# An FFT filter with a bilinear layer behind it on one core: the projection one step later, casts of g behind later products, transform loads three deep

## The chip, the core and the metric

One core of a Trainium2 chip runs the whole program. The metric is the time of one execution in device microseconds (us). The kernel before takes 2731.31 us, the median of three runs (2729.96 to 2734.04).

Engines are named as in the profile: PE is TensorE's matmul, PEld its weight load, DVE is VectorE, ACT is ScalarE, POOL is GpSimd, SP is SyncE, which issues most of the DMAs. Each engine works through its own list of instructions in order, and semaphores tie the lists together.

## What is computed

```python
def _attn_ref(x, filt_r, filt_i):          # x: (8, 3072, 256)
    X = np.fft.rfft(x, axis=1)
    F = (filt_r + 1j * filt_i)[None, :, :]
    Y = X * F
    return np.fft.irfft(Y, n=x.shape[1], axis=1).astype(np.float32)

def _moe_ref(x, w_a, w_b, w_out):          # x: (8 * 3072, 256), w_a, w_b: (256, 1536)
    a = x @ w_a
    b = x @ w_b
    return (a * b @ w_out).astype(np.float32)
```

A long convolution along the sequence (a real FFT, a product with a filter, the inverse FFT), then two first layers, multiplied with each other, and a projection back to 256 columns.

## The kernel before

**Numbers in two parts.** Operands of matmuls are of type fp32r, whose mantissa is cut. To keep precision an operand is held as a high part, cast by ACT, and a low part, the rest that POOL (in places DVE) subtracts. One product is then three matmuls: high with high, high with low, low with high. In the code the parts end in `h` and `l` (`gh`, `gl`, `xh`, `xl`).

**The transforms.** 3072 is 128 x 24. Per batch the forward transform has 12 pieces `s1` (a DFT over 128 rows, from tiles `xt` and a table `st`), whose results go out to DRAM (`store_z`), and 16 pieces `s2` (a DFT over 24, from tiles `zt` read back), each with the filter on DVE: four instructions that make `y`, `v` and `y+v`. The inverse has 16 pieces `is1` (from the halves `yh`, `yl` that `split_y` makes) and per chunk two pieces `is2`, whose results are cast into `ah`, `al`, the operand of the first layers.

**The steps.** The loop runs over 8 batches, 6 chunks `c` of 512 rows, and 6 pairs `p` of column blocks of 128: 288 steps. A step is numbered by its slot, 12c + 2p, from 0 to 70 within a batch. In it, seven products of Strassen's scheme (`product`, numbers 1, 2, 5, 6, 7, 3, 4 in this order, six matmuls of 256 columns each) build both first layers in three PSUM banks x, y, z. ACT copies and DVE additions gather them in `c0` (for block f0) and `c1` (for block f1). `parts` multiplies both layers to `g` on DVE; `split` casts it to `gh` (ACT) and subtracts to `gl` (POOL); `project` multiplies the halves with `w_out` into the banks `po0`, `po1`, 12 matmuls for each of f0 and f1. So a step holds 66 matmuls of 256 columns. `store` copies the two `po` banks to `ot` (two DVE copies) when a chunk's last projection is done.

**The order.** It is written out by hand in the step's code below; nothing reorders it. In the middle of a step, between products 6 and 7, stands the projection of the step before's f0, in front of product 4 that of its f1. `plan` and `early` are tables from slots to pieces of the transforms for the next batch: the even slot's `plan` runs after product 3, the odd slot's in the middle of the next step (`after`), and `early` (the casts `split_x`, `split_y`) also in the middle. In batches 1 to 6, `s1` pieces lie in slots 3 to 25, `s2` in 30 to 60, `is1` in 33 to 63; batch 7 has no transforms to prepare but `is2`. In batch 0 the `s1` pieces come twice as densely (slots 14 to 25), behind a start-up that converts the weights (`more_weights`).

**Buffers that matter.** `c0` and `c1` exist once; ACT's copy of product 5 into `c1[:, 1]` (L727) must therefore wait until DVE's `parts` of the step before's f1 (L567) has read `c1`. Bank x alternates between two, y and z exist once. ACT's copy of product 1 (L720) has to be done before product 6 may write into the same bank, that of product 6 (L729) before product 7. `xt`, `st` and `zt` have two buffers each.

Of the kernel before, what the change touches and what calls it, by code (L numbers as in the profile page):

```python
# [22 lines left out]
NP = NF // 2  # L23
# [174 lines left out]
def fft_filter_bilinear_kernel(ctx: ExitStack, tc, x, filt, fny, wa, wb, wo, s1c, gc, fc, fl, ic, sc, s1f, ff, fi, out):  # L198
# [141 lines left out]
    def load_x(b, i):  # L340
        n0, n1 = PAIRS[i]
        xt = later[0].tile([128, 2, D], F32, name="xt", tag="xt", bufs=2)
        nc.sync.dma_start(out=xt, in_=x[b].rearrange("(p n) d -> p n d", n=N2)[:, n0:n1 + 1:n1 - n0])
        held["x", b, i] = xt

    def load_s(b, i):
        st = later[0].tile([128, 2, 2, 128], F32R, name="st", tag="st", bufs=2)
        nc.sync.dma_start(out=f32(st), in_=s1d[i])
        held["s", b, i] = st
# [9 lines left out]
    def s1(b, i):  # L359
        (xh, xl), st = held.pop(("xs", b, i)), held.pop(("s", b, i))  # L360
        ps = ps_f.tile([128, 2, D], F32, name="ps", tag="ff")
        for n in range(2):
            for q, (w, m) in enumerate(((0, xh), (0, xl), (1, xh))):
                nc.tensor.matmul(ps[:, n], st[:, n, w], m[:, n], start=q == 0, stop=q == 2)  # L364
        zh = later[0].tile([128, 2, D], F32R, name="zh", tag="zh")
        zl = later[0].tile([128, 2, D], F32R, name="zl", tag="zl")
        nc.scalar.copy(out=zh, in_=ps)
        nc.vector.tensor_tensor(out=zl, in0=ps, in1=f32(zh), op=ALU.subtract)
        held["zs", b, i] = zh, zl
# [15 lines left out]
    def load_z(b, i):  # L385
        zt = later[0].tile([128, 2, 2, D], F32R, name="zt", tag="zt")
        for h, r in ((0, 128), (1, 96)):
            zv = zd[b][h].rearrange("(j q) n d -> j (q n) d", q=4)[2 * i:2 * i + 2]
            nc.sync.dma_start(out=f32(zt[0:r, h]), in_=zv.rearrange("j p d -> p j d"))
        held["z", b, i] = zt  # L390
# [12 lines left out]
    def s2(b, i):  # L403
        zt, fr, fm = held.pop(("z", b, i)), filts[2 * (i % 2)], filts[2 * (i % 2) + 1]
        ps = ps_f.tile([128, 2, D], F32, name="ps", tag="ff")
        turn(i, fct, flt, zt[:, 0], zt[0:96, 1], ps)
        y = later[0].tile([128, 2, D], F32, name="y", tag="y")
        v = later[0].tile([128, 2, D], F32, name="v", tag="v", bufs=1)
        nc.vector.scalar_tensor_tensor(out=y, in0=ps, scalar=sct[:, 0:1], in1=fr, op0=ALU.mult, op1=ALU.mult)  # L409
# [10 lines left out]
    def split_y(b, i):  # L420
        y = held["y", b, i]
        yh = later[0].tile([128, 2, D], F32R, name="yh", tag="yh", bufs=1)
        yl = later[0].tile([128, 2, D], F32R, name="yl", tag="yl", bufs=1)
        nc.scalar.copy(out=yh, in_=y)
        nc.gpsimd.tensor_tensor(out=yl, in0=y, in1=f32(yh), op=ALU.subtract)
        held["y", b, i] = yh, yl

    def is1(b, i):
        ps = ps_f.tile([128, 2, D], F32, name="ps", tag="ff")
        turn(i, ict, ict, *held.pop(("y", b, i)), ps[0:96])  # L430
        t = later[0].tile([96, 2, D], F32, name="t", tag="t", bufs=1)
# [132 lines left out]
    def parts(r, g, tag):  # L564

        gt = moe[0].tile([128, 2, 256], F32, name="g", tag="g" + tag)
        nc.vector.tensor_tensor(out=gt, in0=g[:, :, 0], in1=g[:, :, 1], op=ALU.mult)  # L567
        gh = moe[0].tile([128, 2, 256], F32R, name="gh", tag="gh" + tag)
        gl = moe[0].tile([128, 2, 256], F32R, name="gl", tag="gl" + tag)
        r[tag] = gh, gl, gt  # L570

    def split(r, tag):
        gh, gl, gt = r[tag]
        nc.scalar.copy(out=gh, in_=gt)  # L574
# [24 lines left out]
    with tc.manual_schedule():  # L599
# [56 lines left out]

        last, after = None, []
        for b in range(B):
# [15 lines left out]
            if b + 1 < B:  # L674
                at(o, start_batch, b + 1)
                for i in range(2):
                    at(o, load_x, b + 1, i)
                for i in range(2):
                    at(o, load_s, b + 1, i)
                for i in range(NI):  # L680
# [4 lines left out]
                    at(t + 3 if b == 0 else t + 4, store_z, b + 1, i)  # L685
                    if i + 2 < NI:
                        at(t + 2 if b == 0 else t + 3, load_s, b + 1, i + 2)
                        at(t + 2, load_x, b + 1, i + 2)
                t = 26 if b == 0 else 28
                for i in range(2):  # L690
                    at(t - 2, load_f, i)
                at(t, load_z, b + 1, 0)
                at(t, load_z, b + 1, 1)
                for i in range(NJ):
                    t = 30 + 2 * i
                    at(t, s2, b + 1, i)
                    if i + 2 < NJ:
                        at(t, load_z, b + 1, i + 2)
                    if i + 2 < NJ:
# [13 lines left out]
            for c in range(NC):  # L713
                for p in range(NP):
                    slot = NF * c + 2 * p
                    r = {"at": (b, c, p)}
                    bx, by, bz = bank("x"), bank("y"), bank("z")
                    c0 = moe[0].tile([128, 2, 2, 256], F32, name="c0", tag="c0")
                    product(b, c, p, 1, bx, True)
                    nc.scalar.copy(out=c0[:, 0], in_=bx)  # L720
                    product(b, c, p, 2, by, True)
                    if last:
                        parts(last, last["c1"], "f1")
                    nc.vector.tensor_tensor(out=c0[:, 0], in0=by, in1=c0[:, 0], op=ALU.add)
                    product(b, c, p, 5, bz, True)
                    c1 = r["c1"] = moe[0].tile([128, 2, 2, 256], F32, name="c1", tag="c1")
                    nc.scalar.copy(out=c1[:, 1], in_=bz)  # L727
                    product(b, c, p, 6, bx)
                    nc.scalar.copy(out=c0[:, 1], in_=bx)  # L729
                    if last:  # L730
                        split(last, "f1")
                    for what, at_slot in after:
                        run(what, at_slot)
                    run(early, slot)
                    if last:
                        project(last, 0)
                    product(b, c, p, 7, bx)
# [3 lines left out]
                    parts(r, c0, "f0")  # L741
                    split(r, "f0")
                    run(plan, slot)
                    if last:
                        project(last, 1)
                        if p == 0:
                            store(*last["at"][:2])
                    product(b, c, p, 4, bx)
                    nc.scalar.copy(out=c1[:, 0], in_=bx)  # L749
                    after = [(plan, slot + 1), (early, slot + 1)]  # L750
                    if p == NP - 1:
                        del held["t", b, c]
                    last = r
        parts(last, last["c1"], "f1")
        split(last, "f1")
        project(last, 0)
        project(last, 1)
        store(*last["at"][:2])

# [33 lines left out]
```

## Time and profile before

| | |
|---|---|
| median of three runs | 2731.31 us |
| the profiled execution itself | 2729.53 us |
| its span in the trace | 2727.7 us |
| PE busy | 2611.6 us, 96% of the span |
| DVE busy | 1779.0 us, 65% |
| ACT busy | 1362.5 us, 50% |
| POOL busy | 1234.9 us, 45% |
| granted TensorE clock, mean | 0.986 |

Matmuls are pipelined: a matmul of 256 columns is listed with 0.28 us, but the next one starts 0.117 us after it. PE's idle time in the trace counts only from the modelled end of the matmul before, so a step's loss is better read from its length than from the idle times.

### The profile page before, as it was taken

The page shows a single profiled execution, that of the slowest core. Times are in us where ns is not written, and L with a number is a line of the kernel's source. Part 1 is how long each engine was busy: PE and PEld are TensorE (multiplying, and loading weights), DVE is VectorE, ACT ScalarE, POOL GpSimd, SP SyncE. Part 2 cuts the span into 40 slices and gives each one's busy share as a digit, 9 for nine tenths or more (in the row PEclk, how much of TensorE's full clock was granted, in tenths as well). Part 3 has the DMA queues.
Part 4 walks back from the last instruction along what each step waited for, and adds up shares of the span by engine and source line. Part 5 has one row for each costly group of instructions (what it writes and reads, how often), then busy time and mean ns, then how long its engine had stood idle before and what let it go on. Part 6 is the DMA issues. An engine that isn't in the chain of part 4 may idle for free.

```text
span 2727.7 us, 53145 instructions
## 1 busy us (share of the span) xinstructions
PE 2611.6 (96%) x20920; PEld 2522.9 (92%) x20920; DVE 1779.0 (65%) x2552; ACT 1362.5 (50%) x2483; POOL 1234.9 (45%) x948
## 2 busy tenths in 40 slices
PE   5688999999999999999999999999999999999999
PEld 2388999999999999999999999999999999999998
DVE  6674676557765577556775567655776557755555
ACT  4454455545545454555455545455454555544443
POOL 4464444444444444444444544454444444533433
PEclk7899999999999999999999999999999999999999
DMA  8435442344414443243432344234441444310100
GB/s 267 141 110 187 150 135 67 111 159 123 131 52 144 138 131 106 82 146 128 141 101 82 132 150 139 75 101 161 129 130 51 143 136 132 112 46 20 40 20 17
DMA packets 206813, 311.27 MB, mean 114 GB/s; under 512 B 20673, under 2 KB 120578, under 8 KB 206482
## 3 DMA queue, kind: packets, MB, share of 16 engines
q1 hardware_dynamic: 149986, 228.16, 26.6%
q10 hardware_dynamic: 56576, 79.71, 8.5%
q8 instruction: 164, 2.69, 0.4%
q14 instruction: 87, 0.71, 0.1%
HBM read 202.93 MB, written 108.45 MB: 114 GB/s over the span
## 4 chain that ended last, share of the span: by engine, by line
PE 80%; DVE 9%; ACT 4%; issue 3%; DMA 2%; ACTq 1%; POOL 1%; SPq 0%; POOLq 0%; DVEq 0%
PE x L556 27%; PE po L587 26%; PE z L556 13%; PE y L556 6%; PE ps L525 3%; DVE g L567 3%; PE ps L364 2%; PE ps L398 2%; PE ps L399 2%; DVE v L411 1%; ACT c L729 1%; DVE c L740 1%; ACT gh L574 1%; DVE c L738 1%; DVE y L409 1%
## 5 line engine op out<-in xcount | busy, mean ns | idle before, releaser
L575 POOL TENSOR_TENSOR gl<-g,gh 128x512 fp32r<-128x512 f32 x576 | 757.3, 1315 | 1296.8 <-ACT gh L574 1247.5
L567 DVE TENSOR_TENSOR g<-c 128x512 f32<-128x512 f32 x576 | 553.5, 961 | 266.9 <-ACT c L749 216.6
L574 ACT CAST gh<-g 128x512 fp32r<-128x512 f32 x576 | 359.9, 625 | 702.2 <-DVE g L567 699.4
L587 PE MATMUL po<-woh,gl 128*128 128x256 f32 x2304 | 650.5, 282 | 14.4 <-POOL gl L575 14.4
L587 PE MATMUL po<-woh,gh 128*128 128x256 f32 x2304 | 658.0, 286 | 0.7 <-ACT gh L574 0.2
L587 PE MATMUL po<-wol,gh 128*128 128x256 f32 x2304 | 645.6, 280 | 0.0
L587 PEld LDWEIGHTS po<-woh,gl 128*128 128x128 f32 x2304 | 434.4, 189 | 20.6 <-POOL gl L575 20.5
L587 PEld LDWEIGHTS po<-woh,gh 128*128 128x128 f32 x2304 | 435.4, 189 | 19.2 <-DVE ot L595 10.1
L587 PEld LDWEIGHTS po<-wol,gh 128*128 128x128 f32 x2304 | 435.4, 189 | 6.6
L738 DVE TENSOR_TENSOR c<-x,c 128x512 f32<-128x512 f32 x288 | 198.3, 689 | 316.0 <-PE x L556 314.0
L556 PE MATMUL x<-ah,wah 128*128 128x256 f32 x1152 | 334.5, 290 | 41.5 <-ACT c L729 21.7
L727 ACT COPY c<-z 128x512 f32<-128x512 f32 x288 | 169.3, 588 | 392.0 <-DVE g L567 265.7
L556 PE MATMUL x<-ah,wbl 128*128 128x256 f32 x1152 | 323.9, 281 | 0.0
L556 PE MATMUL x<-al,wbh 128*128 128x256 f32 x1152 | 323.8, 281 | 0.0
L556 PE MATMUL x<-al,wah 128*128 128x256 f32 x1152 | 323.6, 281 | 0.0
L556 PE MATMUL x<-ah,wbh 128*128 128x256 f32 x1152 | 323.3, 281 | 0.0
L556 PE MATMUL x<-ah,wal 128*128 128x256 f32 x1152 | 322.9, 280 | 0.0
L556 PEld LDWEIGHTS x<-ah,wah 128*128 128x128 f32 x1152 | 218.0, 189 | 56.9 <-ACT c L729 30.9
L556 PEld LDWEIGHTS x<-al,wah 128*128 128x128 f32 x1152 | 218.9, 190 | 0.0
L556 PEld LDWEIGHTS x<-ah,wal 128*128 128x128 f32 x1152 | 218.1, 189 | 0.0
L556 PEld LDWEIGHTS x<-ah,wbl 128*128 128x128 f32 x1152 | 217.7, 189 | 0.0
L556 PEld LDWEIGHTS x<-ah,wbh 128*128 128x128 f32 x1152 | 217.7, 189 | 0.0
(120 smaller groups left out, 5980.4 us busy)
## 6 DMA issues: line engine op xcount, KB each, us to landing
filt<-in_filt SPq DMA_DIRECT2D x336, 128.0 KB, 2.8
z<-zh ACTq DMA_DIRECT2D x112, 256.0 KB, 2.4
zt<-z SPq DMA_DIRECT2D x112, 256.0 KB, 2.9
td<-t ACTq DMA_DIRECT2D x128, 192.0 KB, 2.1
out<-ot SPq DMA_DIRECT2D x48, 512.0 KB, 2.7
tt<-td SPq DMA_DIRECT2D x47, 512.0 KB, 4.1
xt<-in_x SPq DMA_DIRECT2D x84, 256.0 KB, 2.9
st<-s1d SPq DMA_DIRECT2D x84, 256.0 KB, 2.7
```

Of the source, the lines that this page charges most:

```text
L364: nc.tensor.matmul(ps[:, n], st[:, n, w], m[:, n], start=q == 0, stop=q == 2)
L398: nc.tensor.matmul(ps[:, j:2], w[:, 0], hi[:, j:2], start=True, stop=False)
L399: nc.tensor.matmul(ps[:, j:2], wl[:, 0], lo[:, j:2], start=False, stop=True)
L409: nc.vector.scalar_tensor_tensor(out=y, in0=ps, scalar=sct[:, 0:1], in1=fr, op0=ALU.mult, op1=ALU.mult)
L525: nc.tensor.matmul(ps[:, n], tt[:, n, 128 * k:128 * k + 128], gt[:, n], start=True, stop=True)
L556: nc.tensor.matmul(bank[:, k], w[:, m], v[:, n], start=first and k == 0 and q == 0, stop=q == 2, skip_group_check=True)
L567: nc.vector.tensor_tensor(out=gt, in0=g[:, :, 0], in1=g[:, :, 1], op=ALU.mult)
L574: nc.scalar.copy(out=gh, in_=gt)
L575: nc.gpsimd.tensor_tensor(out=gl, in0=gt, in1=f32(gh), op=ALU.subtract)
L587: nc.tensor.matmul(o, g[:, n], w[p][:, f], start=p == 0 and f == 0 and n % 2 == 0 and q == 0, stop=p == NP - 1 and f == 1 and q == 2, skip ...
L727: nc.scalar.copy(out=c1[:, 1], in_=bz)
L738: nc.vector.tensor_tensor(out=c1[:, 1], in0=bx, in1=c1[:, 1], op=ALU.add)
```

## The change

The projection lags further: where step r held the projections of r-1 (f0 in the middle, f1 near the end), it now holds f1 of step r-2 in the middle and f0 of step r-1 near the end. `split` of f0 is moved from the end of its own step to behind product 2 of the next; `split` of f1 is moved behind the middle's transform pieces and behind the projection there. `c1` gets two buffers. `store` moves from the end of a chunk's first step to the middle of its second. The loads `xt`, `st` and the two halves of `zt` (now separate tiles) share a ring of six buffers of 2 KB and are issued three pieces ahead instead of two; `zh`, `y` and `zl`, `v`, `t` share two rings of two (`e1`, `e2`), `yh`, `yl` the buffers of `xh`, `xl`.

```diff
@@ load_x, load_s
-        xt = later[0].tile([128, 2, D], F32, name="xt", tag="xt", bufs=2)
+        xt = later[0].tile([128, 2, D], F32, name="xt", tag="ld", bufs=6)
...
-        st = later[0].tile([128, 2, 2, 128], F32R, name="st", tag="st", bufs=2)
+        st = later[0].tile([128, 2, 2, 128], F32R, name="st", tag="ld", bufs=6)
@@ load_z
-        zt = later[0].tile([128, 2, 2, D], F32R, name="zt", tag="zt")
+        zt = []
         for h, r in ((0, 128), (1, 96)):
+            zt.append(later[0].tile([r, 2, D], F32R, name=f"zt{'hl'[h]}", tag="ld", bufs=6))
             zv = zd[b][h].rearrange("(j q) n d -> j (q n) d", q=4)[2 * i:2 * i + 2]
-            nc.sync.dma_start(out=f32(zt[0:r, h]), in_=zv.rearrange("j p d -> p j d"))
+            nc.sync.dma_start(out=f32(zt[h]), in_=zv.rearrange("j p d -> p j d"))
@@ s2, is1
-        v = later[0].tile([128, 2, D], F32, name="v", tag="v", bufs=1)
+        v = later[0].tile([128, 2, D], F32, name="v", tag="e2")
...
-        t = later[0].tile([96, 2, D], F32, name="t", tag="t", bufs=1)
+        t = later[0].tile([96, 2, D], F32, name="t", tag="e2")
@@ parts, split
+        r[tag] = gt
+
+    def split(r, tag):
+        gt = r[tag]
         gh = moe[0].tile([128, 2, 256], F32R, name="gh", tag="gh" + tag)
         gl = moe[0].tile([128, 2, 256], F32R, name="gl", tag="gl" + tag)
-        r[tag] = gh, gl, gt
-
-    def split(r, tag):
-        gh, gl, gt = r[tag]
+        r[tag] = gh, gl
@@ the plan of the loads
-                    if i + 2 < NI:
-                        at(t + 2 if b == 0 else t + 3, load_s, b + 1, i + 2)
-                        at(t + 2, load_x, b + 1, i + 2)
+                    if i + 3 < NI:
+                        at(t + 2 if b == 0 else t + 3, load_x, b + 1, i + 3)
+                        at(t + 2 if b == 0 else t + 3, load_s, b + 1, i + 3)
...
-                    if i + 2 < NJ:
-                        at(t, load_z, b + 1, i + 2)
+                    if i + 3 < NJ:
+                        at(t, load_z, b + 1, i + 3)
@@ the step
+                    c1 = r["c1"] = moe[0].tile([128, 2, 2, 256], F32, name="c1", tag="c1", bufs=2)
...
                     product(b, c, p, 2, by, True)
-                    if last:
-                        parts(last, last["c1"], "f1")
+                    if prev:
+                        split(prev[-1], "f0")
+                        parts(prev[-1], prev[-1]["c1"], "f1")
...
                     nc.scalar.copy(out=c0[:, 1], in_=bx)
-                    if last:
-                        split(last, "f1")
                     for what, at_slot in after:
                         run(what, at_slot)
                     run(early, slot)
-                    if last:
-                        project(last, 0)
+                    if len(prev) == 2:
+                        one = prev.pop(0)
+                        project(one, 1)
+                        if one["at"][2] == NP - 1:
+                            store(*one["at"][:2])
+                    if prev:
+                        split(prev[-1], "f1")
                     product(b, c, p, 7, bx)
...
                     parts(r, c0, "f0")
-                    split(r, "f0")
                     run(plan, slot)
-                    if last:
-                        project(last, 1)
-                        if p == 0:
-                            store(*last["at"][:2])
+                    if prev:
+                        project(prev[-1], 0)
@@ behind the loop
+        one, r = prev
+        split(r, "f0")
+        parts(r, r["c1"], "f1")
+        split(r, "f1")
+        project(one, 1)
+        project(r, 0)
+        project(r, 1)
+        store(*r["at"][:2])
```

How the rows stand on the engines, at the places that matter. First ACT in the step of slot 48 of batch 3 (c = 4, p = 0), from the copy of product 4 before it to the one at its end; L720/L722, L727/L729, L729/L731 and L749/L751 copy products 1, 5, 6 and 4. Before:

```order
L749 COPY c1_16024<-x_15996 128x512
L720 COPY c0_16128<-x_16125 128x512
L727 COPY c1_16153<-z_16127 128x512
L729 COPY c0_16128<-x_16125 128x512
L574 CAST gh_16144<-g_16142 128x512
L432 COPY t_16167<-ps_16164 96x512
L434 DMA td_13403<-t_16167 96x2x256
L424 CAST yh_16170<-y_16094 128x512
L574 CAST gh_16202<-g_16200 128x512
L749 COPY c1_16153<-x_16125 128x512
```

And after, the same step:

```order
L751 COPY c1_16046<-x_16042 128x512
L722 COPY c0_16175<-x_16172 128x512
L576 CAST gh_16190<-g_16135 128x512
L729 COPY c1_16176<-z_16174 128x512
L731 COPY c0_16175<-x_16172 128x512
L433 COPY t_16214<-ps_16211 96x512
L435 DMA td_13435<-t_16214 96x2x256
L425 CAST yh_16217<-y_16140 128x512
L576 CAST gh_16233<-g_16194 128x512
L751 COPY c1_16176<-x_16172 128x512
```

The cast for f0 went from in front of the last copy of its step to between the copies of products 1 and 5 of the next; the cast for f1 went behind the transform's `t` and `yh`.

POOL around the step of slot 46 (p = 5) and the next, with the two subtractions `al` of the chunk's `is2`. Before:

```order
L575 TENSOR_TENSOR gl_16016<-g_16013,gh_16015 128x512
L545 TENSOR_TENSOR al_15684<-t_15921,ah_15683 128x512 x2
L425 TENSOR_TENSOR yl_16056<-y_15965,yh_16055 128x512
L575 TENSOR_TENSOR gl_16088<-g_16085,gh_16087 128x512
L575 TENSOR_TENSOR gl_16145<-g_16142,gh_16144 128x512
```

After:

```order
L577 TENSOR_TENSOR gl_16061<-g_16005,gh_16060 128x512
L546 TENSOR_TENSOR al_15727<-t_15966,ah_15726 128x512 x2
L426 TENSOR_TENSOR yl_16102<-y_16010,yh_16101 128x512
L577 TENSOR_TENSOR gl_16118<-g_16064,gh_16117 128x512
L577 TENSOR_TENSOR gl_16191<-g_16135,gh_16190 128x512
```

On POOL the kinds stand in the same sequence; the `gl` ahead of `al` is now an f0, the one behind `yl` an f1.

DVE at the start of a chunk's second step (slot 50), where L567/L568 is `parts`, L595/L597 the copies of `store` and L738/L743 the addition of product 7. Before:

```order
L567 TENSOR_TENSOR g_16200<-c0_16128 128x512
L409 SCALAR_TENSOR_TENSOR y_16209<-ps_16206,sct_114,filt2_120 128x512
L411 SCALAR_TENSOR_TENSOR v_16210<-ps_16206,sct_114,filt3_121 64x512 x2
L417 TENSOR_TENSOR y_16209<-y_16209,v_16210 128x512
L595 COPY ot_16233<-po0_15566 128x512
L595 COPY ot_16233<-po1_15567 128x512
L567 TENSOR_TENSOR g_16261<-c1_16153 128x512
L724 TENSOR_TENSOR c0_16247<-y_16245,c0_16247 128x512
L738 TENSOR_TENSOR c1_16272<-x_16244,c1_16272 128x512
```

After:

```order
L568 TENSOR_TENSOR g_16251<-c0_16175 128x512
L410 SCALAR_TENSOR_TENSOR y_16256<-ps_16253,sct_114,filt2_120 128x512
L412 SCALAR_TENSOR_TENSOR v_16257<-ps_16253,sct_114,filt3_121 64x512 x2
L418 TENSOR_TENSOR y_16256<-y_16256,v_16257 128x512
L568 TENSOR_TENSOR g_16310<-c1_16176 128x512
L727 TENSOR_TENSOR c0_16291<-y_16289,c0_16291 128x512
L597 COPY ot_16349<-po0_15656 128x512
L597 COPY ot_16349<-po1_15657 128x512
L743 TENSOR_TENSOR c1_16292<-x_16288,c1_16292 128x512
```

The two copies of `store` went from ahead of `parts` of f1 to behind it and behind the addition of product 2.

## Rows read from the trace of the kernel before

**Rows 1.** Page: PE's busy time, share and count; granted clock in 40 slices.

```profile
PE 2611.6 (96%) x20920; PEld 2522.9 (92%) x20920; DVE 1779.0 (65%) x2552; ACT 1362.5 (50%) x2483; POOL 1234.9 (45%) x948
...
PEclk7899999999999999999999999999999999999999
```

**Rows 2.** Waits of PE over the span: us in total, times, longest.

```profile
PE x L556 <- ACT c L729: 21.7, 44, 1.3
PE po L587 <- POOL gl L575: 14.4, 23, 0.8
PE x L556 <- ACT c L720: 12.9, 15, 2.2
...
PE ps L364 <- POOL xl L356: 4.5, 4, 2.8
```

**Rows 3.** Windows, batch 3: slots 36, 38, 40, 48, 50, 60, 62, 64; then slots 36-46.

```profile
core 0: us, PE busy (x) PEld busy (x) DVE busy (x) ACT busy (x) POOL busy (x), PEclk, DMA share, GB/s
1286.66:1296.54 9.88, 9.27 (x73) 8.66 (x71) 8.10 (x10) 4.41 (x9) 6.60 (x5) 1.00 0.35 105
1296.54:1306.48 9.94, 9.22 (x72) 8.46 (x71) 8.04 (x12) 4.32 (x9) 3.90 (x3) 1.00 0.48 154
1306.48:1315.18 8.70, 8.70 (x73) 8.50 (x71) 6.86 (x10) 4.42 (x9) 3.90 (x3) 1.00 0.69 218
1343.10:1353.38 10.28, 9.28 (x73) 8.68 (x71) 8.50 (x11) 4.44 (x9) 7.00 (x5) 1.00 0.34 101
1353.38:1363.34 9.96, 9.25 (x73) 8.50 (x71) 8.05 (x12) 4.35 (x9) 3.90 (x3) 1.00 0.50 157
1399.95:1410.21 10.26, 9.26 (x72) 8.67 (x71) 8.51 (x11) 4.45 (x9) 6.98 (x5) 1.00 0.07 21
1410.21:1419.89 9.68, 9.00 (x71) 8.15 (x69) 7.79 (x11) 4.19 (x8) 3.88 (x3) 1.00 0.21 74
1419.89:1428.10 8.21, 8.21 (x70) 8.10 (x69) 3.96 (x5) 4.01 (x8) 2.58 (x2) 1.00 0.13 31
...
1286.66:1343.10 56.44, 55.10 (x439) 52.94 (x438) 43.66 (x62) 28.76 (x53) 26.37 (x21) 1.00 0.44 136
```

**Rows 4.** Timeline, batch 3, slots 46 to 48: start, us, instruction, idle before and releaser.

```profile
1336.67 0.59 ACT L727 COPY c<-z 128x512 f32<-128x512 f32 x1 [1.69 <-DVE g L567]
...
1339.12 0.59 ACT L538 CAST ah<-ps 128x512 fp32r<-128x512 f32 x1 [0.38 <-PE po L587]
...
1341.49 3.08 POOL L545 TENSOR_TENSOR al<-t,ah 128x512 fp32r<-128x512 f32 x2 [1.87 <-ACT ah L544]
1344.54 1.29 POOL L425 TENSOR_TENSOR yl<-y,yh 128x512 fp32r<-128x512 f32 x1
1345.79 1.72 POOL L575 TENSOR_TENSOR gl<-g,gh 128x512 fp32r<-128x512 f32 x1
...
1346.30 1.75 DVE L567 TENSOR_TENSOR g<-c 128x512 f32<-128x512 f32 x1
...
1347.56 0.38 PE L587 MATMUL po<-woh,gl 128*128 128x256 f32 x1 [0.74 <-POOL gl L575]
...
1348.14 0.59 ACT L727 COPY c<-z 128x512 f32<-128x512 f32 x1 [3.04 <-DVE g L567]
```

**Rows 5.** Timeline of DVE, batch 3, slot 38: the copies of the store.

```profile
1299.28 1.29 DVE L595 COPY ot<-po 128x512 f32<-128x512 f32 x2
```

**Rows 6.** Windows, batch 2, the steps of slots 16 and 24.

```profile
873.45:881.95 8.50, 8.50 (x75) 8.50 (x74) 4.29 (x6) 4.40 (x9) 3.85 (x3) 1.00 0.60 210
...
909.64:919.41 9.77, 8.77 (x74) 8.56 (x73) 5.28 (x8) 4.74 (x9) 5.65 (x5) 1.00 0.21 82
```

**Rows 7.** Timeline of ACT, batch 2, slots 22 to 24.

```profile
910.43 0.62 ACT L574 CAST gh<-g 128x512 fp32r<-128x512 f32 x1 [2.07 <-DVE g L567]
...
911.81 0.59 ACT L749 COPY c<-x 128x512 f32<-128x512 f32 x1 [0.76 <-PE y L556]
```

**Rows 8.** Waits of PE between 140 and 290 us, the start-up of batch 0.

```profile
PE x L556 <- ACT c L720: 6.3, 6, 2.2
```

**Rows 9.** Timeline of ACT, batch 7, slot 18: the copy of product 1.

```profile
2501.30 0.59 ACT L720 COPY c<-x 128x512 f32<-128x512 f32 x1
```

More of the change, by code (lines that the diff above doesn't have):

```diff
@@ L364, in s1 @@
                 nc.tensor.matmul(ps[:, n], st[:, n, w], m[:, n], start=q == 0, stop=q == 2)
-        zh = later[0].tile([128, 2, D], F32R, name="zh", tag="zh")
-        zl = later[0].tile([128, 2, D], F32R, name="zl", tag="zl")
+        zh = later[0].tile([128, 2, D], F32R, name="zh", tag="e1")
+        zl = later[0].tile([128, 2, D], F32R, name="zl", tag="e2")
         nc.scalar.copy(out=zh, in_=ps)
@@ L405, in s2 @@
         ps = ps_f.tile([128, 2, D], F32, name="ps", tag="ff")
-        turn(i, fct, flt, zt[:, 0], zt[0:96, 1], ps)
-        y = later[0].tile([128, 2, D], F32, name="y", tag="y")
-        v = later[0].tile([128, 2, D], F32, name="v", tag="v", bufs=1)
+        turn(i, fct, flt, zt[0], zt[1], ps)
+        y = later[0].tile([128, 2, D], F32, name="y", tag="e1")
+        v = later[0].tile([128, 2, D], F32, name="v", tag="e2")
         nc.vector.scalar_tensor_tensor(out=y, in0=ps, scalar=sct[:, 0:1], in1=fr, op0=ALU.mult, op1=ALU.mult)
@@ L421, in split_y @@
         y = held["y", b, i]
-        yh = later[0].tile([128, 2, D], F32R, name="yh", tag="yh", bufs=1)
-        yl = later[0].tile([128, 2, D], F32R, name="yl", tag="yl", bufs=1)
+        yh = later[0].tile([128, 2, D], F32R, name="yh", tag="xh", bufs=1)
+        yl = later[0].tile([128, 2, D], F32R, name="yl", tag="xl", bufs=1)
         nc.scalar.copy(out=yh, in_=y)
@@ L580, in project @@
         b, c, p = r["at"]
-        gh, gl = (t.rearrange("p h (n m) -> p (h n) m", n=2) for t in r.pop(f"f{f}")[:2])
+        gh, gl = (t.rearrange("p h (n m) -> p (h n) m", n=2) for t in r.pop(f"f{f}"))
         if p == 0 and f == 0:
@@ L655, in fft_filter_bilinear_kernel @@
         streaming.append(True)
-        last, after = None, []
+        prev, after = [], []
         for b in range(B):
@@ L675, in fft_filter_bilinear_kernel @@
                 at(o, start_batch, b + 1)
-                for i in range(2):
+                for i in range(3):
                     at(o, load_x, b + 1, i)
-                for i in range(2):
                     at(o, load_s, b + 1, i)
@@ L691, in fft_filter_bilinear_kernel @@
                     at(t - 2, load_f, i)
-                at(t, load_z, b + 1, 0)
-                at(t, load_z, b + 1, 1)
+                for i in range(3):
+                    at(t, load_z, b + 1, i)
                 for i in range(NJ):
@@ L721, in fft_filter_bilinear_kernel @@
                     product(b, c, p, 2, by, True)
-                    if last:
-                        parts(last, last["c1"], "f1")
+                    if prev:
+                        split(prev[-1], "f0")
+                        parts(prev[-1], prev[-1]["c1"], "f1")
                     nc.vector.tensor_tensor(out=c0[:, 0], in0=by, in1=c0[:, 0], op=ALU.add)
                     product(b, c, p, 5, bz, True)
-                    c1 = r["c1"] = moe[0].tile([128, 2, 2, 256], F32, name="c1", tag="c1")
                     nc.scalar.copy(out=c1[:, 1], in_=bz)
@@ L752, in fft_filter_bilinear_kernel @@
                         del held["t", b, c]
[L753 to L758, printed above, removed]
+                    prev.append(r)
+        one, r = prev
[6 more added lines that the diff above has]
+        store(*r["at"][:2])
 def kernel(x, filt_r, filt_i, moe_w_a, moe_w_b, moe_w_out):
```

## The prediction, made before the changed kernel was run

> **What bounds the kernel now.** I read the page's busy times first: PE is busy for 96% of the span, at full clock after the start [rows 1]. No work is taken off PE by the change, so it can win only PE's idle time, and the question is where that lies. The list of PE's waits names four kinds [rows 2]: product 7 waits for ACT's copy of product 6 (L729, 44 times), a projection waits for POOL's `gl` (23 times), product 6 waits for ACT's copy of product 1 (L720, 15 times), `s1` waits for POOL's `xl` (4 times). Third, lengths of steps. Where `s2` and `is1` both run, an undisturbed step takes 8.70 us (slot 40) and the last one, with `is1` alone, 8.21 (slot 64). The first two steps of chunks 3, 4 and 5 are longer [rows 3]: slot 36 by 1.18, 38 by 1.24, 48 by 1.58, 50 by 1.26, 60 by 1.56, and 62 (no `s2` either) by 9.68 - 8.21 = 1.47. That is 8.29 us in a batch; the pattern repeats in batches 0 to 6, which makes 58.0 us. These six steps hold 42 of the 44 waits for L729 and 21 of the 23 for `gl`. A wait costs more than its idle time: the `gl` wait of 0.74 in slot 48 starts a matmul at 1347.56 where 1346.66 would have been due, and the next comes 0.22 later instead of 0.117; so wait plus about 0.27.
>
> **Why they wait.** Slot 48 is typical [rows 4]. (a) `gl`: POOL ends the two `al` at 1344.57, `yl` at 1345.83, `gl` at 1347.51; the projection needed it at 1346.66. `al` starts late because of a chain on ACT in slot 46: the copy of product 5 begins at 1336.67 after waiting for DVE's `parts`, then come the copy of product 6, the cast `gh`, the transform's `t`, and only at 1339.12 the `ah` from which DVE and ACT build what `al` needs. (b) L729: ACT's copy of product 5 starts at 1348.14, after 3.04 idle, when DVE's `g` (1346.30 to 1348.05) has released the single `c1`; the copy of product 6 stands behind it. In a chunk's second step, DVE's two store copies (1.29 us) stand ahead of that `g` as well [rows 5].
>
> **Term 1, chunks 3 to 5.** The second `c1` ends the wait in (b): ACT copies product 5 when PE has made it, and the copy of product 6 has the projection of 12 matmuls (1.4 us) and the `is1` (0.46) to hide its 0.59. The store copies leave the place ahead of `g`. Of the 8.29 us a batch, the `gl` part is 0.62 + 1.01 + 1.01 (waits 0.35, 0.74, 0.74 plus 0.27 each), the L729 part the other 5.65, or 39.5 over seven batches; I count it as gone. The `gl` part, 18.5 over seven batches, is less sure, because POOL's sequence does not change: behind the two `al` and `yl` there is still a `gl` that the middle projection of the next step needs at the same place. What changes is when `al` starts. Without the wait for `c1` the copy of product 5 can start at about 1335.7 instead of 1336.67, and the cast `gh` no longer stands ahead of `t` and `ah`, so `ah` comes 1.1 us earlier, and `gl` ends at 1346.4 or sooner against 1346.66 (in slot 36, where the ACT wait was shorter, I find 0.66 against a lateness of 0.46). In addition that `gl` took 1.72 beside DVE's `g`, where `yl` took 1.29, and it would now be nearly over when `g` starts. So margin exists, but of some tenths. I take 16.5 of 18.5: term 1 is -56, with bounds -58 and -39.
>
> **Term 2, product 6 in chunks 1 and 2, batches 1 to 6.** In slot 24 of batch 2 the step takes 9.77 us, 1.28 more than the like step of slot 16 [rows 6]. ACT's list there is cast `gh` of f0 (which waits for DVE's `parts`, 2.07 idle), three DMA issues of `store_z` until 911.77, the copy of product 4 at 911.81, then that of product 1, on which product 6 waits [rows 7]. The cast is taken out of this place; the DMA issues then need only `zl`, long done, and run before product 4 ends. What is late next is DVE's `parts` of f0, which still reads the single `c0` before ACT may copy product 1 into it; in this slot it ended at about 910.3, when product 1 ended, and product 6 is due 1.4 us later. Nine waits of L720 (12.9 - 6.3 of the start-up [rows 2, 8]) with 0.27 each make 9.0; losses of about 0.2 in each of three steps a batch, below what the list shows, another 3.6. I take -11 of these 12.6; bounds 0 and -13.
>
> **Term 3, the start-up of batch 0.** Between 140 and 290 us L720 costs 6.3 us in six waits and `xl` 4.5 in four [rows 2, 8]. The cast out of the way of L720 and the loads one piece earlier both help, but the conversions of the weights keep all engines busy in this stage, and `xl` also waits behind `al`. I take half with restarts, -8; bounds +5 and -16.
>
> **Term 4, the ends.** The first steps have one projection less, the tail 12 matmuls (1.4 us) more, which cover the casts that PE waited for at the end. -1, between -2 and +2.
>
> **What costs nothing, and its cover.** The cast for f0 waits on ACT behind the copy of product 1, and `c0` already had to be free of `parts` for that copy, so it adds no wait. `gl` of f0 is now needed in the step in which it is cast. In batch 7, where steps are shortest, the copy of product 1 ends at 2501.89 [rows 9]; 0.62 for the cast [rows 7] and 1.29 for the subtraction give 2503.8. The projection needs it after 50 matmuls of the step that began at 2500.40, at 2506.3: 2.4 us in hand. The cast for f1 now waits for the middle projection of r-2 (the one buffer of `gh`); behind it on ACT stand only DMA issues and the copy of product 4, 2 us later. The store's copies wait for that projection's end; the next projection starts into `po0` 12 matmuls (products 7 and 3) and `s2` later (1.9 us in chunks 3 to 5, 1.4 elsewhere), and the first copy takes 0.65, the second is needed half a projection later still. On SP the loads keep their order among others; each waits for a reader one piece older than before, so nothing is queued behind a longer wait. The shared rings `e1`, `e2` alternate `v` and `t` and give each the one buffer that it had.
>
> **The sum.** -56 - 11 - 8 - 1 = -76. The profiled execution took 2729.5, so 2653.5 by its own time; the median of the runs lies 1.8 above that execution, so 2655.
>
> **The rivals.** *The `gl` wait stays.* If `al` starts less early than I think, 18.5 us of term 1 remain: 2655 + 16.5 = 2672. For it: POOL's unchanged sequence and the margin of tenths. Against: two delays on ACT go at once.
> *DVE becomes the bound of chunks 3 to 5.* A chunk's six steps hold 43.7 us of DVE work [rows 3]. Twelve of these instructions are `g`, of which the one of slot 48 took 1.75 beside POOL's `gl` [rows 4]; with 0.69 alone and a mean near 1.0, all at 1.75 would add 9, giving 52.7 of the 54.0 that PE needs (56.44 less the losses of slots 36 and 38). DVE would then fit only on average, and the second steps with the store copies would keep their losses, 21 times about 1.25: 26, so 2681. The cast for f0 now puts a POOL subtraction next to `parts` of f1 in every step, which is what speaks for it. The Trainium skill (SBUF — State Buffer, "Who interferes with whom") says that a DVE instruction with two SBUF inputs and a GpSimd instruction that reads SBUF exclude one another for the whole length of the first. The two rows of slot 48 agree with that; by this rule alone every meeting would cost DVE up to a whole subtraction, and the time would be this rival's.
> *Slower: the projection of f0 waits in every step.* If the chain copy of product 1, `gh`, `gl` took 2.4 us longer than its rows say, all 288 steps would stall, each for the restart of 0.27 even at a wait near nothing: 78 us, the whole gain. From a wait of 0.3 on, the time is 2655 + 288 x 0.57 = 2819. Against it stands that POOL is idle for 55% of the span.
> *No effect.* The waits move to something that I don't see, for instance `parts` of f0 ahead of `c0`: near 2731.
>
> **Chances and range.** The forecast 0.73, the `gl` wait 0.12, DVE 0.08, slower 0.04, no effect 0.03. All gains at their bounds give -58 - 13 - 16 - 2 = -89, 2642; the range starts at 2640. Upwards it takes in the `gl` wait and DVE with a few us for term 3: 2688. A measurement can tell about 0.2% (5.5 us) from no change. Faster 0.93, same 0.03, slower 0.04.
>
> **What would show it.** Right: in batches 0 to 6 the steps of slots 36, 38, 48, 50, 60 take 8.7 us and slot 62 takes 8.2; L729 and L720 nearly vanish from PE's waits; ACT's copy of product 5 waits for PE, not for DVE's `g`; `ah` starts about 1 us sooner after product 5. The `gl` rival shows as waits in the third matmul of the middle projection in slots 36, 48, 60; DVE's as `g` near 1.7 in most steps with waits for DVE or L720 in chunks 3 to 5; the slower one as waits for `gl` in the late projection of batch 7. I am wrong if the long steps remain with another releaser, or if new losses appear in steps of 7.8 or 8.5 us that now have none.

## The result and the profile after

The changed kernel takes 2652.05 us (median of four runs, 2649.73 to 2653.44) against 2730.81 of the kernel before in the same comparison: a ratio of 0.9709, 95% interval 0.9692 to 0.9725. The forecast was 2655, range 2640 to 2688. The profiled execution took 2651.09, which is 78.4 us less than that of before.

From the page of the changed kernel, its busy times and granted clock, which answer to [rows 1]:

```profile
PE 2575.3 (97%) x20920; PEld 2513.0 (95%) x20920; DVE 1832.4 (69%) x2552; ACT 1404.3 (53%) x2483; POOL 1256.8 (47%) x948
...
PEclk7899999999999999999999999999999999999999
```

The same number of counted instructions on each engine in a shorter span; DVE's busy time is 53 us longer, most of it in `parts` (mean 1041 ns against 961). The windows of the changed kernel (length, then busy time and count by engine, clock, DMA): first the steps of slots 36, 38, 40, 48, 50, 60, 62 of batch 3 and of slots 16 and 24 of batch 2, in the order of [rows 3] and [rows 6]; then everything behind the start-up.

```profile
1248.50:1257.23 8.73, 8.73 (x73) 8.53 (x71) 7.36 (x9) 4.56 (x8) 7.05 (x6) 1.00 0.41 122
1257.23:1265.92 8.69, 8.69 (x72) 8.49 (x71) 8.47 (x12) 4.49 (x8) 4.16 (x3) 1.00 0.50 154
1265.92:1274.62 8.70, 8.70 (x73) 8.50 (x72) 7.79 (x10) 4.49 (x8) 4.15 (x3) 1.00 0.74 241
1302.53:1311.26 8.73, 8.73 (x72) 8.53 (x71) 7.36 (x9) 4.57 (x8) 7.06 (x6) 1.00 0.41 119
1311.26:1319.95 8.69, 8.69 (x72) 8.49 (x71) 8.47 (x12) 4.49 (x8) 4.16 (x3) 1.00 0.49 151
1356.57:1365.30 8.73, 8.73 (x73) 8.53 (x72) 7.36 (x9) 4.57 (x8) 7.05 (x6) 1.00 0.08 23
1365.30:1373.52 8.22, 8.22 (x71) 8.11 (x70) 8.02 (x11) 4.49 (x8) 4.14 (x3) 1.00 0.24 86
846.43:854.92 8.49, 8.49 (x74) 8.49 (x73) 4.15 (x6) 4.60 (x8) 3.84 (x3) 1.00 0.64 194
882.19:890.69 8.50, 8.50 (x75) 8.50 (x73) 4.86 (x6) 4.60 (x8) 7.02 (x6) 1.00 0.30 114
...
290.00:2640.00 2350.00, 2350.00 (x19568) 2328.95 (x19567) 1639.43 (x2242) 1259.88 (x2223) 1104.99 (x818) 1.00 0.35 110
```

All six long steps of chunks 3 to 5 have the length of an undisturbed one, slot 24 too, and between 290 and 2640 us PE is never idle. What is left lies in the start-up and at the very end. DVE is at 8.47 of 8.69 us in a chunk's second step (slots 38, 50).

The timeline of slots 46 to 48 of batch 3, to be read beside [rows 4]:

```profile
1295.24 0.59 ACT L729 COPY c<-z 128x512 f32<-128x512 f32 x1 [0.31 <-PE z L557]
...
1297.40 0.59 ACT L539 CAST ah<-ps 128x512 fp32r<-128x512 f32 x1 [0.38 <-PE ps L526]
...
1299.77 3.07 POOL L546 TENSOR_TENSOR al<-t,ah 128x512 fp32r<-128x512 f32 x2 [3.19 <-ACT ah L545]
1302.80 1.30 POOL L426 TENSOR_TENSOR yl<-y,yh 128x512 fp32r<-128x512 f32 x1
1303.93 0.71 DVE L418 TENSOR_TENSOR y<-y,v 128x512 f32<-128x512 f32 x1
1304.05 1.75 POOL L577 TENSOR_TENSOR gl<-g,gh 128x512 fp32r<-128x512 f32 x1
...
1305.83 1.77 DVE L568 TENSOR_TENSOR g<-c 128x512 f32<-128x512 f32 x1 [1.19 <-POOL gl L577]
...
1306.08 0.28 PE L589 MATMUL po<-woh,gl 128*128 128x256 f32 x1
```

ACT's copy of product 5 now waits for PE alone. The step of slot 46 began at 1292.92, so `al` starts 6.85 us after it; before it was 8.01 (a step from 1333.48). `gl` ends at 1305.80 and is used at 1306.08: 0.28 us in hand. And a wait that I had not named: DVE's `parts` of f1 stands 1.19 us for POOL's `gl`, because `g` has one buffer and its last reader, the cast and subtraction of f1, has moved back.

### The profile page after: what moved, and what is told of

It reads as the page before. It is cut to its first block, busy times and chain, and to the rows that moved or that the text cites. A ratio compares the mean times of both kernels' runs of the same rounds, so it can differ in the third digit from the quotient of the medians.

```text
span 2649.3 us, 53618 instructions
## 1 busy us (share of the span) xinstructions
PE 2575.3 (97%) x20920; PEld 2513.0 (95%) x20920; DVE 1832.4 (69%) x2552; ACT 1404.3 (53%) x2483; POOL 1256.8 (47%) x948
## 4 chain that ended last, share of the span: by engine, by line
PE 93%; DVE 3%; DMA 2%; issue 1%; POOL 1%; ACT 1%; ACTq 0%; SPq 0%; DVEq 0%; POOLq 0%
PE po L589 30%; PE x L557 30%; PE z L557 15%; PE y L557 8%; PE ps L526 3%; PE ps L364 2%; PE ps L399 2%; PE ps L400 2%; DMA x<-in_x 0%; DVE s L312 0%; DMA z<-z 0%; DVE e L256 0%; DMA raw<-in_wa 0%; DVE v L486 0%; DVE e L283 0%
## 5 line engine op out<-in xcount | busy, mean ns | idle before, releaser
L577 POOL TENSOR_TENSOR gl<-g,gh 128x512 fp32r<-128x512 f32 x576 | 789.1, 1372 | 903.0 <-ACT gh L576 893.5
L568 DVE TENSOR_TENSOR g<-c 128x512 f32<-128x512 f32 x576 | 599.6, 1041 | 290.7 <-ACT c L751 177.5
L751 ACT COPY c<-x 128x512 f32<-128x512 f32 x288 | 169.0, 587 | 782.4 <-PE x L557 776.5
L743 DVE TENSOR_TENSOR c<-x,c 128x512 f32<-128x512 f32 x288 | 197.9, 687 | 220.9 <-PE x L557 200.6
L557 PE MATMUL x<-ah,wah 128*128 128x256 f32 x1152 | 325.5, 283 | 13.3 <-ACT c L722 4.5
L546 POOL TENSOR_TENSOR al<-t,ah 128x512 fp32r<-128x512 f32 x96 | 137.5, 1455 | 170.9 <-ACT ah L545 170.9
```

What stands on the lines that cost most here:

```text
L546: nc.gpsimd.tensor_tensor(out=al[:, 3 + i:5 + i], in0=t[:, i:i + 2], in1=f32(ah[:, 3 + i:5 + i]), op=ALU.subtract)
L557: nc.tensor.matmul(bank[:, k], w[:, m], v[:, n], start=first and k == 0 and q == 0, stop=q == 2, skip_group_check=True)
L577: nc.gpsimd.tensor_tensor(out=gl, in0=gt, in1=f32(gh), op=ALU.subtract)
L743: nc.vector.tensor_tensor(out=c1[:, 1], in0=bx, in1=c1[:, 1], op=ALU.add)
```

## The experiments

All were compared with the kernel before on the same chip, like the changed kernel; the medians of the kernel before lie between 2729.2 and 2730.8 us, so times of different comparisons are set beside one another as they are.

**One part alone (e1): the second `c1`.** To the kernel before only this is added, and room made for it by letting `yl` share with `xl` as `yh` with `xh`:

```diff
-                    c1 = r["c1"] = moe[0].tile([128, 2, 2, 256], F32, name="c1", tag="c1")
+                    c1 = r["c1"] = moe[0].tile([128, 2, 2, 256], F32, name="c1", tag="c1", bufs=2)
-        yh = later[0].tile([128, 2, D], F32R, name="yh", tag="yh", bufs=1)
+        yh = later[0].tile([128, 2, D], F32R, name="yh", tag="xh", bufs=1)
...
```

> The kernel before with a second buffer of c1 as the only change to the layer's work (yh, yl move into the buffers of xh, xl to make room). Theory (the single c1 made the waits for the copy of product 6): the 39.5 us of those waits go, some of the gl waits too since ah comes about 0.6 us earlier, the losses of product 6 in chunks 1 and 2 stay; up to 8 us come back where the middle projection of a chunk's second step now reaches po before the store's first copy: 2731 - 58 + 6 + 8 = 2687, between 2676 and 2695. Rival (the store's copies and DVE's backlog made the waits, not the buffer): only the first steps of a chunk gain, 21 x 0.53 = 11 us: 2720, and slots 38, 50, 62 stay at 9.7 to 10.0 us.

2680.34 us, ratio 0.9816 (0.9800 to 0.9833): 50 us less than before. Windows of slots 48 and 50 of batch 3:

```profile
1322.24:1331.40 9.16, 9.03 (x73) 8.63 (x71) 7.85 (x11) 4.97 (x9) 6.37 (x5) 1.00 0.40 116
1331.40:1340.08 8.68, 8.68 (x73) 8.48 (x71) 7.51 (x11) 4.53 (x8) 3.88 (x3) 1.00 0.57 181
```

The second step of the chunk loses nothing although the store's copies stand where they stood, so the rival is out, and beside the second `c1` moving the store is worth nothing. The first step loses 0.46, the rest of the `gl` wait. ACT in slot 46, which began at 1312.63:

```profile
1316.13 0.62 ACT L574 CAST gh<-g 128x512 fp32r<-128x512 f32 x1
1316.65 0.58 ACT L432 COPY t<-ps 96x512 f32<-96x512 f32 x1
...
1317.62 0.59 ACT L538 CAST ah<-ps 128x512 fp32r<-128x512 f32 x1 [0.38 <-ACT t L432]
```

`ah` starts 4.99 us into the step; before it was 5.64, in the changed kernel 4.48. The cast of f1 still stands ahead of it.

**The opposite (e2): a single `c1` in the changed kernel** (`bufs=2` taken away).

> The changed kernel with a single c1. Theory (the second buffer carries most of term 1): the copy of product 5 waits again for parts of f1, which in slot 48 ended 2.9 us after product 5; product 7 then waits about 1.6 us in slots 36, 48, 60 and up to 1 us in 38, 50, 62: 21 x 1.9 + 21 x 0.8 = 57, 2700, between 2680 and 2715. Rival (the order of casts and store carries it): 2652 to 2660.

2767.24 us, ratio 1.0143 (1.0125 to 1.0161): slower than the kernel before, and far outside the range. Slot 60 of batch 3, timeline of DVE, ACT and PE, then the windows of the step and of its middle:

```profile
1425.92 1.75 DVE L568 TENSOR_TENSOR g<-c 128x512 f32<-128x512 f32 x1 [1.16 <-POOL gl L577]
...
1427.76 0.58 ACT L729 COPY c<-z 128x512 f32<-128x512 f32 x1 [4.47 <-DVE g L568]
...
1425.94 0.39 PE L589 MATMUL po<-woh,gl 128*128 128x256 f32 x1 [0.95 <-POOL gl L577]
...
1428.88 0.58 PE L557 MATMUL x<-ah,wah 128*128 128x256 f32 x1 [1.50 <-ACT c L731]
```
```profile
1421.26:1435.76 14.50, 12.05 (x72) 11.30 (x71) 10.31 (x14) 4.59 (x9) 8.38 (x6) 0.76 0.05 15
1425.80:1433.00 7.20, 5.56 (x27) 5.17 (x28) 4.18 (x5) 2.69 (x5) 3.84 (x4) 0.67 0.10 27
```

And slot 48 of batch 2, for comparison:

```profile
1032.39:1044.12 11.73, 9.25 (x73) 8.57 (x71) 8.76 (x12) 4.59 (x9) 8.45 (x6) 1.00 0.26 75
```

The wait of `parts` for `gl` passes through the single `c1` to ACT (4.47 us idle) and on to product 7. Two waits of PE, 0.95 and 1.50, fall within 4 us, and behind them the granted clock is 0.67 over 7.2 us, a mean of the full and the half level (2.4 and 1.2 GHz). The step takes 14.50 instead of 8.7 us. The same pair of waits (0.97 and 1.51) in slot 48 of batch 2 left the clock at 1.00 and cost 3.0. In this trace 8 of the 14 steps of slots 48 and 60 are of the longer kind. It is that of the slowest execution (2776.99), 10 us above the median.

**Is it the one buffer of `g`? (e2b)** The same kernel with `g` of f1 twice:

```diff
-        gt = moe[0].tile([128, 2, 256], F32, name="g", tag="g" + tag)
+        gt = moe[0].tile([128, 2, 256], F32, name="g", tag="g" + tag, bufs=2 if tag == "f1" else 1)
```

> The changed kernel with a single c1 and two buffers of g of f1. e2 (single c1) took 2767, slower than the kernel before, where 2700 was expected. Theory (in the changed order parts of f1 waits for POOL to have read the one buffer of g, 1.16 us in slot 60, and with a single c1 that wait passes through ACT's copies to product 7, in slots 48 and 60 far enough that the clock falls): parts starts 1.2 us sooner, slots 12, 24, 36, 48, 60 lose 1.2 or more less, the clock stays up: 2767 - 7 x (2 x 2.5 + 3 x 1.2) = 2707, between 2690 and 2728. Rival (DVE's own backlog, lengthened beside POOL, makes e2 slow): 2750 to 2770.

2711.66 us (ratio 0.9937, 0.9922 to 0.9952), 55.6 us less than with one `g`. Beside the changed kernel the steps of a batch were longer by 15 to 20 us in all with one `g`, and are by 9 with two (11 in batch 0); what remains, 1.8 in slots 48 and 60 and 1.2 in some others, comes with the single `c1`, the only other difference.

**The cast of f0 back, in two places (e3, e3b).** First behind the late projection, so that the one buffer of `gh` does:

```diff
-                        split(prev[-1], "f0")
...
                         project(prev[-1], 0)
+                    split(r, "f0")
...
```

> The changed kernel with the cast of f0 back in front of ACT's copy of product 4 (behind the late projection, so that one buffer of gh does). Theory (this place of the cast made product 6 wait in chunks 1 and 2): slot 24 loses about 1.3 us again, slots 22, 26, 28 about 0.2 each, in six batches, 12 us, and a few in batch 0: 2664, between 2657 and 2672. Rival (those losses went for another reason, such as the second c1): 2652 within 3.

2661.16 us (0.9747, 0.9732 to 0.9761): 9 us return, but in batches 1 to 6 slots 22, 26, 28 lose nothing, and slot 24 loses 0.45 in one batch and nothing in five. In the trace the 9 us lie elsewhere: mainly 0.4 in slot 0 of batches 1 to 7, 0.4 in the other first steps of chunks of batch 7, and some 4 in the start-up. The time lies in the range, but neither theory holds as stated: here the cast stands behind the DMA issues of `store_z`, before it stood in front of them. So e3b puts it exactly there, with two buffers of `gh` and `gl` of f0 from the transforms' pool:

```diff
                     parts(r, c0, "f0")
+                    if later:
+                        split(r, "f0")
                     run(plan, slot)
...
```

> The changed kernel with the cast of f0 back exactly where it stood, at the end of its own step and in front of the plan's DMA issues on ACT (gh and gl of f0 have two buffers, taken from the transforms' pool). e3 put it behind those issues and only 9 us came back, with 0.5 where 1.3 was lost before. Theory (the cast delays product 6 because the DMA issues of store_z, 1.3 us, queue behind it): slot 24 loses 1.3, slots 22, 26, 28 some 0.2 each, 2 us in each of batches 1 to 6, and about 8 elsewhere as in e3: 2652 + 12 + 5 = 2669, between 2662 and 2676. Rival (the losses of chunks 1 and 2 went for another reason): no more than in e3, 2661 within 3.

2671.9 us (0.9786, 0.9773 to 0.9799). POOL, DVE and ACT at the start of slot 24 of batch 3, and that step's window:

```profile
1204.49 2.55 POOL L546 TENSOR_TENSOR al<-t,ah 128x512 fp32r<-128x512 f32 x2 [5.47 <-ACT ah L545]
1206.98 1.76 POOL L356 TENSOR_TENSOR xl<-xt,xh 128x512 fp32r<-128x512 f32 x1
...
1205.77 1.82 DVE L568 TENSOR_TENSOR g<-c 128x512 f32<-128x512 f32 x1
...
1207.62 0.62 ACT L578 CAST gh<-g 128x512 fp32r<-128x512 f32 x1 [1.50 <-DVE g L568]
1207.68 0.33 ACTq L373 DMA_DIRECT2D z<-zh  x1
1208.04 0.44 ACTq L374 DMA_DIRECT2D z<-zl  x1
1208.52 0.48 ACTq L376 DMA_DIRECT2D z<-zh  x1
1209.04 0.59 ACT L756 COPY c<-x 128x512 f32<-128x512 f32 x1 [0.80 <-PE y L557]
```
```profile
1206.89:1216.69 9.80, 8.79 (x74) 8.59 (x73) 5.82 (x7) 4.93 (x9) 6.86 (x6) 1.00 0.21 80
```

The 1.3 us of [rows 6] are back in batches 3 to 6; slots 22, 26 and 28 lose some 0.5, 0.2 and 0.7. The cast waits for DVE, and the issues, 1.3 us of ACT's time, can't start before it. A third thing has to come together with these two, which neither the prediction nor the expectations name: DVE's `parts` of f0, on which the cast waits, takes 1.82 us beside POOL's `al` and `xl` instead of 0.69. In batches 1 and 2, where it took 0.69, slot 24 loses 0.33 and 0.11. It is the same in the kernel before: 1.82 and 1.3 lost in five of batches 1 to 6, 0.69 and 0.16 lost in batch 3. In the changed kernel this `parts` takes 1.85 in batches 3 and 5, and slot 24 loses nothing. In e3 the one batch that loses 0.45 is the one with 1.85. So of the 1.3, about 0.45 remains with the cast behind the issues, and 0.85 is the issues held behind the cast.

**The cast without the lag (e5).** The kernel before with the second `c1` and the cast of f0 behind product 2 of the next step, while f0 is still projected in that step's middle:

```diff
-                    split(r, "f0")
...
                     if last:
+                        split(last, "f0")
                         parts(last, last["c1"], "f1")
...
```

> The kernel before with the second c1 and the cast of f0 behind product 2 of the next step, but the projections not lagging. Theory (the cast can only move because the projection lags): from the rows of batch 7 gl of f0 ends at 2503.85 where the middle projection wants it at 2503.45; the some 54 steps without transform pieces in the middle lose 0.4 + 0.27 each, 36 us, the others have 0.5 us more and lose little: 2687 - 13 + 36 = 2710, between 2695 and 2730. Rival (the lag is not needed): 2655 to 2665.

2707.17 us (0.9916, 0.9901 to 0.9931), 27 us worse than the second `c1` alone. A step without transform pieces in batch 7 takes 8.25 us instead of 7.78: PE waits 0.2 for `gl` at the third matmul of the projection, plus the restart. From slot 6 of batch 7:

```profile
2422.11 0.39 PE L587 MATMUL po<-woh,gl 128*128 128x256 f32 x1 [0.21 <-POOL gl L575]
```

So without the lag the cast of f0 can't be moved into the next step for nothing. The rest of the `gl` wait belongs to the cast of f1: `ah` starts 4.99 us into slot 46 here as in e1, where that cast stands ahead of it, and 4.48 and 4.37 in e3 and e3b, where it stands behind. In those two slots 36, 48 and 60 are whole (8.73 and 8.71) although the cast of f0 is back.

**The loads two pieces ahead (e6)**, as before, in the changed kernel (in the plan of `load_x`, `load_s`, `load_z` every `i + 3` is `i + 2` again, and two pieces instead of three at the start).

> The changed kernel with the loads of x, the table and z issued two pieces ahead as before (in the ring of six). Theory (term 3: the earlier loads help batch 0 alone): the waits of xh for the transfer of xt return in batch 0, +4, between 0 and +8: 2656; nothing in batches 1 to 7. Rival (the depth of the loads does nothing, the start-up gain came from the casts): 2652 within 2.

2652.2 us (0.9714, 0.9699 to 0.9729) against 2652.05: no difference. Between 190 and 290 us PE waits 4.2 us with either depth, 3.1 for `xl` and 1.1 for `xh` here, 3.0 and 1.2 with three. The rival was right.

**How much room the new chain has.** POOL's subtraction for f0 is done twice (e7), and with a 3 in the place of the 2 three times (e8):

```diff
-        nc.gpsimd.tensor_tensor(out=gl, in0=gt, in1=f32(gh), op=ALU.subtract)
+        for _ in range(2 if tag == "f0" else 1):
+            nc.gpsimd.tensor_tensor(out=gl, in0=gt, in1=f32(gh), op=ALU.subtract)
```

> The changed kernel with POOL's subtraction for f0 done twice, so gl of f0 comes 1.3 us later and POOL has 374 us more work. Theory (2.4 us in hand): 1.1 us remain, batch 7 shows no wait for gl, steps of chunks 3 to 5 lose a few tenths at most: 2652 to 2662. Rival (the chain of cast and subtraction, or the clash of POOL and DVE, has no room): over 2690.

> The changed kernel with POOL's subtraction for f0 done three times. By the 2.4 us in hand of the prediction, two more (2.6) go past it by 0.2: the 24 steps of batch 7 without is2 lose 0.2 + 0.27 each where with one more (e7) they lost nothing, some 5 such steps in each other batch too, and slots 36, 48, 60 lose 1 to 2 us more through DVE, as in e7: 2671 + 24 x 0.4 + 35 x 0.4 + 21 x 1.5 = 2726, between 2695 and 2745. Rival (the reading of 2.4 is too small, or batch 7 is held by another chain): batch 7 as in e7, under 2695.

2671.04 us (0.9783, 0.9770 to 0.9799) and 2745.3 (1.0058, 1.0041 to 1.0074). A step of slot 18 or 16 in batch 7, with one, two and three subtractions, from the windows of the three kernels:

```profile
2422.00:2429.78 7.78, 7.78 (x69) 7.78 (x67) 3.41 (x5) 3.49 (x6) 2.57 (x2) 1.00 0.00 0
```
```profile
2430.23:2438.01 7.78, 7.78 (x68) 7.78 (x67) 3.41 (x5) 3.49 (x6) 3.88 (x3) 1.00 0.27 95
```
```profile
2495.76:2503.92 8.16, 8.04 (x68) 7.84 (x67) 3.97 (x5) 3.50 (x6) 5.12 (x4) 1.00 0.21 78
```

1.3 us more cost such a step nothing, 2.6 us cost it 0.38 (0.12 of it idle time, 0.26 the restart). That is where the 2.4 us in hand end. The 19 us of the first kernel lie between the theory (up to 10) and the rival (over 38) and come from elsewhere: 1.0 in slots 48 and 60 of seven batches make 14, and 2.7 the longer tail. The second kernel lies just past the upper end of its range (2745): batches 1 to 6 lose some 10 us each beside the changed kernel, batch 7 loses 16. POOL and DVE in slot 46 of the first kernel:

```profile
1303.18 2.99 POOL L578 TENSOR_TENSOR gl<-g,gh 128x512 fp32r<-128x512 f32 x2 [2.87 <-ACT gh L576]
```
```profile
1303.39 1.63 DVE L418 TENSOR_TENSOR y<-y,v 128x512 f32<-128x512 f32 x1
1304.94 1.77 DVE L568 TENSOR_TENSOR g<-c 128x512 f32<-128x512 f32 x1
```

Beside the two subtractions DVE's addition `y+v` takes 1.63 (0.69 in slot 46 of the changed kernel) and `g` 1.77. DVE reaches the `al` of `is2` 1.2 us late, POOL's `al` starts 7.99 us into the step instead of 6.85, and the 0.28 in hand for the `gl` of f1 is gone.

**A faster version (e9).** What the changed kernel still loses in one place is slot 22 of batch 0, 16.66 us long: `xl` stands behind `al` on POOL, and ACT's next `xh` waits for the `s1` that still reads the one buffer. POOL and PE there:

```profile
242.69 2.50 POOL L546 TENSOR_TENSOR al<-t,ah 128x512 fp32r<-128x512 f32 x2 [4.12 <-ACT ah L545]
245.14 1.72 POOL L356 TENSOR_TENSOR xl<-xt,xh 128x512 fp32r<-128x512 f32 x1
...
246.91 0.58 PE L364 MATMUL ps<-xl,st 128*128 128x256 f32 x1 [2.68 <-POOL xl L356]
```

So `xh` and `xl` (and with them `yh` and `yl`) get two buffers, `is2` of that slot comes behind the split of x, and the last step's cast of f0 is issued in its own step:

```diff
-        xh = later[0].tile([128, 2, D], F32R, name="xh", tag="xh", bufs=1)
+        xh = later[0].tile([128, 2, D], F32R, name="xh", tag="xh", bufs=2)
...
+                    if b == 0 and c == 1:
+                        early.setdefault(12 * c + 9, []).append((is2, nb, ncx, 1))
+                    else:
...
                         project(prev[-1], 0)
+                    if (b, c, p) == (B - 1, NC - 1, NP - 1):
+                        split(r, "f0")
```

> The changed kernel with two buffers of xh and xl, in batch 0 the second is2 of chunk 2 issued behind the split of x, and the last step's cast of f0 at once. Theory (what is left lies in batch 0's slots 20 to 24, where xl stands behind al on POOL, and in the last 1.3 us): slot 22 loses about 1 instead of 6.7, its slow clock included, the tail nothing: -7, 2645, between 2641 and 2650. Rival (the weights and the density of pieces in batch 0 hold it): 2650 to 2653.

2645.71 us (2643.7 to 2648.52), ratio 0.9691 (0.9678 to 0.9705), the fastest kernel here: its slowest run is below the changed kernel's fastest (2649.73), though the intervals of the two ratios overlap. The window of slot 22 in the changed kernel and in this one:

```profile
235.19:251.85 16.66, 12.75 (x89) 12.35 (x87) 7.75 (x12) 7.32 (x13) 9.35 (x8) 0.80 0.48 161
```
```profile
235.92:246.00 10.08, 10.08 (x88) 10.08 (x87) 5.84 (x11) 7.23 (x13) 5.00 (x5) 1.00 0.59 172
```

6.6 us in the step, with the clock at 1.00 instead of 0.80; the median moved by 6.3. Whether the buffers or the place of `is2` gave it was not tried apart. The tail did not gain: its wait of 0.9 for `gl` of f0 became one of 0.8 for that of f1.

## Why the prediction was right, and where its reasons were not

By the lengths of steps (the 12 matmuls that went from slot 2 of batch 0 to the end counted at 0.117 us each in both places), the two profiled executions differ as follows, with the forecast in brackets: chunks 3 to 5 -57.6 (-56), the other slots of batches 1 to 6 -13.0 (-11), the start-up of batch 0 -8.9 (-8), the tail -1.4 (-1). The first streaming step began 2.5 us later than before, in a stage that the change does not touch. The sum is -78.4, as measured. Terms 1 and 2, 70.6 of it, are borne out place by place; in the start-up some luck is in the agreement (term 3).

*Term 1* held, also in its narrow part: `al` starts 1.16 us sooner, 1.1 was read, and 0.28 remains of "some tenths". What it gave to the store's move is wrong: with the second `c1` alone the second steps were whole. `c1` alone is worth 50 of the 58, and the other 7.7, in slots 36, 48 and 60, come with the later cast of f1. Wrong too is that `gl` is lengthened by `g` and would be shorter once it ends before `g` starts: it does end before (1305.80 and 1305.83) and still took 1.75. What ran beside it was `y+v`, at 1303.93.

*Term 2* held in size, and in mechanism only when the two casts-back runs are taken together: the cast must stand in front of the issues for the full loss. The prediction named both but did not say that the order between them decides, and it took the late `parts` as given: slot 24 loses 1.3 only where that instruction takes 1.82 instead of 0.69.

*Term 3* came near the measured size by a cause that is half wrong: the depth of the loads gives nothing (e6). Of the 8.9 us, 3.7 lie in slots 0 and 8 of batch 0, which took 15.47 and 12.74 us before and 12.72 and 11.82 after; in the trace of e6, whose instructions in these two slots are those of the changed kernel, they took 14.69 and 14.59. So there executions of like code differ by more than the gain. The late start and the shorter slot 0 also belong together: that step ended at 135.66 after 135.85. The other 5 us, in slots 6 and 14 to 28, are the same in e6. In slots 14, 16, 26 and 28, which hold 3.4 of them, the second `c1` alone (e1) gives nothing, so they come with the rest of the change, whose parts were not tried apart. There the waits that the term named are gone: 1.06 and 0.54 for L720 in slots 26 and 28, 0.82 for `xl` in slot 14. And -8 is not half: the ten waits, 10.8 us, make 13.5 with 0.27 each, half of which is 6.8.

*The rivals.* The `gl` rival was 0.28 us away. DVE did get longer beside POOL, as the rule of the Trainium skill (SBUF — State Buffer, "Who interferes with whom") has it: mean of `g` 961 to 1041 ns, the single one 0.69 us alone and up to 1.85 beside POOL. DVE's work in slots 36 to 46 of batch 3 rose from 43.66 to 49.30 us, below the 52.7 of this rival and inside the 54.03 that the six steps take; e7 shows that one subtraction more tips slots 48 and 60 over. The slower rival exists too: at 2.6 us more the whole gain is gone (2745).

*What the prediction missed.* It took `c1`'s second buffer as the end of one wait. In the changed order it also carries a second one, of `parts` for the single `g`. Without it the same casts and lag cost 37 us against the kernel before. The expectation for that kernel (2700) went by the old waits and so was 67 us short. The forecast was not hurt because the second `c1` hides both; that it would hide this one too was not reasoned, and in this the forecast was lucky.

## What to carry to other kernels

Where an engine is 96% busy, the lengths of like steps beside one another show the loss better than the list of waits: a short wait cost 0.27 us more than its idle time. Before a cast or copy is moved back in time, list every tile that it reads or writes and how many buffers each has; the wait that the move takes away can come back through the tile that it now holds longer. And a reordering that only works with one more buffer should be tried with the buffer alone first: here that was most of the gain.

## What the runs showed of the hardware

A wait of PE costs the idle time that the trace lists and about 0.27 us of restart, in e5 (0.21 idle, a step 0.47 longer) and in e8 (0.12, 0.38) alike; in slot 48 of the kernel before, waits of 0.74 and 0.26 go with a step 1.58 longer. In e2, two waits of 0.95 and 1.50 us within 4 us were followed by a granted clock of 0.67 over 7.2 us in one place and 1.00 in another, so the same stalls cost 3.0 or 5.8 us. DVE instructions with two inputs in SBUF lengthen beside POOL's subtractions, `g` from 0.69 to as much as 1.85 and `y+v` from 0.69 to 1.63, and POOL's from 1.30 to 1.75; with the subtraction tripled, DVE's `parts` has a mean of 1251 ns instead of 1041.
